# Vector-as-weights in four column tiles for two matrix-vector products at the edges of a decode kernel

## The chip, the cores and the metric

The kernel runs on one core of a Trainium2 chip (trn2). The metric is device time in microseconds (us). Before the change the median of the first three runs is 357.5 us (357.15 to 358.15). "Span" is the length of one profiled execution; the reported times are about 1.8 us longer. In the profiles PE is the matrix engine (PEld its weight loads), DVE the vector engine, ACT the scalar engine, and SPq and ACTq are the sync and the scalar engine issuing a transfer. The granted PE clock is the share of full speed at which the PE was let run; "half clock" is 0.50. PSUM (`ps`) is the memory that the matmuls here write to, in banks. "The tail" is what happens after the last big loads land, from about 342 us to the end.

## The reference, cut to what matters

```
q = x @ wq                                   # x: 1 x 512, 32 heads of 128
scores = q . k_cache ; p = softmax(scores)   # 8 KV heads, 32768 keys each
o = p . v_cache                              # 4096 numbers
a = o @ wo                                   # wo: 4096 x 512
b = (silu(x @ w_gate) * (x @ w_up)) @ w_down # w_down: 1792 x 512
g = sigmoid(sum(x * gate_w))
out = g * a + (1 - g) * b                    # 512 numbers, bf16
```

The K and V caches are 134 MB of the 148 MB that the kernel reads, so it is a kernel that streams memory. The products with wo and w_down multiply one vector by a matrix.

## The kernel before

All loads go through one queue into a ring of five slots. The order is wq, K, gate and up weights, K, w_down, then K and V halves in turn, then the last two V halves, then wo in four pieces (of 16, 8, 4 and 4 rows of matmuls). The last V half lands some 10 us before the last piece of wo.

The two products take a 128x128 block of the matrix as weights and one column of the vector as the moving operand. So the output lies down the partitions, as 128 x 4:

```python
# w_down, early in the kernel
for oc in range(OC):                      # OC = 4
    for j in range(FC):                   # FC = 14
        pe.matmul(ps_m[:, M_B0 + oc : M_B0 + oc + 1],
                  wd[:, j, oc * 128 : (oc + 1) * 128], tT[:, j : j + 1],
                  start=(j == 0), stop=(j == FC - 1))
# ... K and V stages cut ...
# wo, the last thing the PE does
for c, n in enumerate(WO_CUT):            # (16, 8, 4, 4)
    pe.wait_ge(sem_ldo[c], 16)            # that piece of wo has landed
    for j in range(j0, j0 + n):
        for oc in range(OC):
            ins = pe.matmul(ps_a[:, oc, :],
                            wo_v[:, j, oc * 128 : (oc + 1) * 128], O2[:, j : j + 1],
                            start=(j == 0), stop=(j == WOJ - 1))
    j0 += n
```

The combine step then works on 128 x 4, and a matmul with the identity and one more copy turn the result into four rows, which the store can write:

```python
dve.scalar_tensor_tensor(res, ps_a, g_col, b_pre, ALU.mult, ALU.add)   # 128 x 4
pe.matmul(ps_r[0:OC, 0:128], res[:, :], ident[:, :], start=True, stop=True)
dve.tensor_copy(row[:, :], ps_r[0:OC, 0:128])                          # 4 x 128
sp.dma_start(out[0, 0, :].rearrange("(c n) -> c n", c=OC), row[:, :])
```

## Time and profile before

| what | value | view |
|---|---|---|
| load queue | 97.2% of 16 engines' span | DMA queues |
| PE, DVE busy | 72%, 56% | page, part 1 |
| chain that ended last | DMA 67%, PE 29% | chain of waits |
| w_down: 56 matmuls | 1.55 us at 57 us | timeline |
| wo: 128 matmuls | 112 in 3.15 us, then a wait, then 16 in 0.58 us | timeline |

The page of the kernel before: granted PE clock and DMA share in 40 slices (tenths), the load queue, and the engines of the chain that ended last.

```profile
PEclk9999678978989896969899896969769987969656
DMA  8999999999999999999999999999999999999991
...
q1 hardware_dynamic: 5768, 148.11, 97.2%
...
DMA 67%; PE 29%; DVE 2%; issue 1%; SPq 0%; DVEq 0%
```

The loads never pause until the last slice. Only what stands behind the last landings can be exposed. The timeline of the tail, in order of time (start us, length us, engine, line, operation, and in brackets the idle time before it and what ended it):

```profile
342.74 3.21 PE L463 MATMUL ps<-ring,ET 128*16 128x512 bf16 x32 [5.41 <-DMA ring<-in_A_v_cache_dram]
...
346.81 1.05 PE L479 MATMUL ps<-osel,pv_sb 128*128 128x4 f32 x8 [0.86 <-DVE pv_sb L719]
...
348.87 3.15 PE L542 MATMUL ps<-O,ring 128*128 128x1 bf16 x112 [0.29 <-DVE O L765]
352.57 0.58 PE L542 MATMUL ps<-O,ring 128*128 128x1 bf16 x16 [0.56 <-DMA ring<-in_A_wo_dram]
353.31 0.22 DVE L769 SCALAR_TENSOR_TENSOR res<-ps,g_col,b_pre 128x4 bf16<-128x4 f32 x1 [4.50 <-PE ps L542]
353.58 0.27 PE L552 MATMUL ps<-ident,res 128*4 128x128 bf16 x1 [0.43 <-DVE res L769]
353.89 0.28 DVE L778 CAST row<-ps 4x128 bf16<-4x128 f32 x1 [0.36 <-PE ps L552]
354.19 0.34 SPq L329 DMA_DIRECT2D out_dram<-row  x1
```

Two paths meet in the tail. One starts where the last V half lands (342.7): P times V, a sum over groups (L479), a short vector chain, then the wo matmuls. The other is the landing of the last piece of wo. The PE had finished 112 of the 128 wo matmuls and sat idle 0.56 us until that piece landed.

### The profile page before, as it was taken

The numbers are of one execution on the slowest core, as the hardware profiler recorded it, in microseconds if no ns is written. First come the engines' busy times: TensorE is split into PE (matmuls) and PEld (weight loads), VectorE is DVE, ScalarE is ACT, GpSimd is POOL, SyncE is SP. The second block draws the span as 40 slices with busy tenths as digits, with TensorE's granted clock in tenths as the row PEclk, the third lists the DMA queues.
The fourth block names the chain that finished last, engine by engine and source line by source line (L and its number), as shares of the span: only waits on it lengthen the run. The fifth ranks groups of instructions, "written<-read, shape, count | busy, mean of one in ns | idle before, by whom it ended". The sixth has DMA issues, their size and how long they took to land.

```text
span 355.8 us, 6082 instructions
## 1 busy us (share of the span) xinstructions
PE 257.5 (72%) x2616; PEld 191.4 (54%) x2616; DVE 198.2 (56%) x372; ACT 14.5 (4%) x36; POOL 5.6 (2%) x22
## 2 busy tenths in 40 slices
PE   0439898869494967868593948868497929678735
PEld 0437887647382736655471828456474618365315
DVE  0239187928383764838392845748365927548401
ACT  1000011000100010000100010000100010000100
POOL 0200000000000000000000000000000000000000
PEclk9999678978989896969899896969769987969656
DMA  8999999999999999999999999999999999999991
GB/s 335 424 404 460 414 438 422 431 437 424 429 438 423 431 433 431 429 435 422 436 429 427 435 429 431 433 426 432 435 422 437 435 422 427 438 427 424 433 386 73
DMA packets 5797, 148.49 MB, mean 417 GB/s; under 512 B 650, under 2 KB 652, under 8 KB 908
## 3 DMA queue, kind: packets, MB, share of 16 engines
q1 hardware_dynamic: 5768, 148.11, 97.2%
q8 instruction: 20, 0.33, 0.4%
q14 instruction: 5, 0.04, 0.0%
q10 hardware_dynamic: 4, 0.00, 0.0%
HBM read 148.11 MB, written 0.00 MB: 416 GB/s over the span
## 4 chain that ended last, share of the span: by engine, by line
DMA 67%; PE 29%; DVE 2%; issue 1%; SPq 0%; DVEq 0%
DMA ring<-in_A_k_cache_dram 55%; PE ps L415 18%; DMA ring<-in_A_wo_dram 12%; PE ps L431 5%; PE ps L463 2%; PE ps L384 2%; DVE ktT L726 1%; PE ps L479 0%; PE ps L398 0%; SPq L317 0%; PE ps L445 0%; PE ps L542 0%; SPq L299 0%; PE ps L552 0%; DVE row L778 0%
## 5 line engine op out<-in xcount | busy, mean ns | idle before, releaser
L726 DVE COPY ktT<-ps 128x1024 bf16<-128x1024 bf16 x256 | 164.2, 685 | 104.4 <-PE ps L415 101.8
L415 PE MATMUL ps<-ident_f,ring 128*128 128x128 f32 x1024 | 164.3, 321 | 57.0 <-DMA ring<-in_A_k_cache_dram 57.0
L415 PEld LDWEIGHTS ps<-ident_f,ring 128*128 128x128 f32 x1024 | 141.0, 167 | 89.5 <-DMA ring<-in_A_k_cache_dram 63.6
L431 PE MATMUL ps<-ktT,qz 128*32 128x512 bf16 x512 | 41.8, 403 | 15.2 <-DVE ktT L726 15.1
L463 PE MATMUL ps<-ring,ET 128*16 128x512 bf16 x512 | 33.4, 406 | 5.4 <-DMA ring<-in_A_v_cache_dram 5.4
L463 PEld LDWEIGHTS ps<-ring,ET 128*16 128x16 bf16 x512 | 13.1, 94 | 22.2 <-DMA ring<-in_A_v_cache_dram 5.5
L431 PEld LDWEIGHTS ps<-ktT,qz 128*32 128x32 bf16 x512 | 7.9, 95 | 28.0 <-DVE ktT L726 24.4
L573 ACT ACTIVATE P<-ps,nbias 128x512 bf16<-128x512 f32 x16 | 10.8, 682 | 273.6 <-DVE nbias L703 273.6
L682 DVE TENSOR_REDUCE pmaxf<-ps 128x1 f32<-128x512 f32 x16 | 11.1, 692 | 11.9 <-PE ps L431 11.9
L479 PEld LDWEIGHTS ps<-osel,pv_sb 128*128 128x128 f32 x64 | 10.0, 237 | 1.7 <-DVE pv_sb L719 1.7
L479 PE MATMUL ps<-osel,pv_sb 128*128 128x4 f32 x64 | 9.6, 274 | 1.0 <-DVE pv_sb L719 0.9
L719 DVE COPY pv_sb<-ps 128x512 f32<-128x512 f32 x8 | 5.5, 682 | 8.3 <-PE ps L463 8.3
L289 POOL PARTITION_ALL_REDUCE gmax<-pmax x8 | 3.0, 373 | 310.5 <-DVE pmax L692 310.5
L445 PE MATMUL ps<-ident,P 128*128 128x128 bf16 x64 | 6.2, 219 | 1.8 <-ACT P L573 1.2
L711 DVE COPY ET<-ps 128x512 bf16<-128x512 bf16 x16 | 6.7, 416 | 1.3 <-PE ps L445 1.3
L384 PEld LDWEIGHTS ps<-xT,ring 128*128 128x128 bf16 x112 | 6.8, 159 | 0.4 <-issue 0.4
L384 PE MATMUL ps<-xT,ring 128*128 128x1 bf16 x112 | 6.9, 198 | 0.0
L359 PE MATMUL ps<-xT,ring 128*128 128x1 bf16 x128 | 3.6, 165 | 4.2 <-DMA ring<-in_A_wq_dram 4.2
L342 PE MATMUL ps<-ones_bf,x_row 1*128 1x1 bf16 x4 | 0.3, 172 | 8.3 <-DMA gw_row<-in_gate_w_dram 8.3
L445 PEld LDWEIGHTS ps<-ident,P 128*128 128x128 bf16 x64 | 4.8, 98 | 2.6 <-ACT P L573 2.4
L359 PEld LDWEIGHTS ps<-xT,ring 128*128 128x128 bf16 x128 | 3.5, 104 | 4.3 <-issue 4.3
L342 PEld LDWEIGHTS ps<-ones_bf,x_row 1*128 1x128 bf16 x4 | 0.2, 113 | 8.3 <-DMA gw_row<-in_gate_w_dram 8.3
(70 smaller groups left out, 38.1 us busy)
## 6 DMA issues: line engine op xcount, KB each, us to landing
ring<-in_A_k_cache_dram SPq DMA_DIRECT2D x16, 4096.0 KB, 43.0
ring<-in_A_v_cache_dram SPq DMA_DIRECT2D x16, 4096.0 KB, 36.9
ring<-in_A_wq_dram SPq DMA_DIRECT2D x1, 4096.0 KB, 13.4
ring<-in_A_wo_dram SPq DMA_DIRECT2D x1, 2048.0 KB, 38.3
ring<-in_B_w_gate_dram SPq DMA_DIRECT2D x1, 1792.0 KB, 26.7
ring<-in_B_w_up_dram SPq DMA_DIRECT2D x1, 1792.0 KB, 30.5
ring<-in_B_w_down_dram SPq DMA_DIRECT2D x1, 1792.0 KB, 43.5
ring<-in_A_wo_dram SPq DMA_DIRECT2D x1, 1024.0 KB, 40.4
```

Of the source, the lines that this page charges most:

```text
L359: ins = pe.matmul(ps_m[:, M_Q0 + h : M_Q0 + h + 1], wq_v[:, c, h * DH : (h + 1) * DH], xT[:, c : c + 1], start=(c == 0), stop=(c == KC - 1),)
L384: ins = pe.matmul(ps_m[:, base + j : base + j + 1], wt[:, c, :].rearrange("d (p j) -> d j p", j=FC)[:, j, :], xT[:, c : c + 1], start=(c = ...
L415: ins = pe.transpose(stb[:, t * 64 : (t + 2) * 64], two.bitcast(FP32), ident_f[:, :])
L431: ins = pe.matmul(ps_sc[f % NSC][32 * c : 32 * c + 32, :], qz[:, g, e, 24 - PB * i : 56 - PB * i], kt[:, e, :], start=(i == 0 and e == 0), ...
L445: ins = pe.transpose(ps_pt[:, (f % 2) * 512 + m * 128 : (f % 2) * 512 + (m + 1) * 128], P[:, f % 2, m * 128 : (m + 1) * 128], ident[:, :],)
L463: ins = pe.matmul(ps_pv[32 * c : 32 * c + 2 * PB, :], ET[:, f % NET, col : col + 2 * PB], src.rearrange("p (i c t) d -> p i c t d", i=NI, ...
L479: ins = pe.matmul(ps_m[:, M_OT + g * HPG : M_OT + (g + 1) * HPG], pv_sb[:, r * DH : (r + 1) * DH], osel[:, r * HPG : (r + 1) * HPG], start ...
L573: act.activation(P[:, f % 2, :], ps_sc[f % NSC], ACT.Exp, bias=nbias[:, f // 2 : f // 2 + 1], scale=SCALE, accum_out=esum[:, f // 2, f % 2 ...
L682: ins = dve.tensor_reduce(pmaxf[:, f : f + 1], ps_sc[f % NSC], AX.X, ALU.max)
L711: dve.tensor_copy(ET[:, f % NET, :], ps_pt[:, (f % 2) * 512 : (f % 2 + 1) * 512]).then_inc(sem_ptc, 1)
L719: dve.tensor_copy(pv_sb[:, :], ps_pv).then_inc(sem_pvc, 1)
L726: dve.tensor_copy(ktT[:, j % NKT, :], pst[j % NST]).then_inc(sem_cp, 1)
```

## The change

The intent: swap the operands of both products. The vector is now the weight, one column wide, and 128 columns of the matrix are the moving operand. The four output blocks run in four column tiles of the PE array, and the output lies in rows, on partitions 0, 32, 64 and 96. The combine step can then write rows, and the transposing matmul and the row copy go away. The combine now works on all 128 partitions though only four hold results, so the PSUM bank of the results is cleared at the start (the `memset` below).

```diff
-        b_pre = T("b_pre", [128, OC], FP32)
-        res = T("res", [128, OC], BF16)
-        row = T("row", [OC, 128], BF16)
+        b_pre = T("b_pre", [128, 128], FP32)
+        res = T("res", [128, 128], BF16)
...
-                sp.wait_ge(sem_row, 1)
+                sp.wait_ge(sem_res, 1)
                 sp.dma_start(
-                    out[0, 0, :].rearrange("(c n) -> c n", c=OC), row[:, :]
+                    out[0, 0, :].rearrange("(c n) -> c n", c=OC), res[0:128:32, :]
...                                       # w_down: the same swap, j now the outer loop
                             ins = pe.matmul(
-                                ps_a[:, oc, :],
+                                ps_a[32 * oc : 32 * oc + 1, :],
+                                O2[:, j : j + 1],
                                 wo_v[:, j, oc * 128 : (oc + 1) * 128],
-                                O2[:, j : j + 1],
...
-                pe.wait_ge(sem_res, 1)
-                pe.matmul(ps_r[0:OC, 0:128], res[:, :], ident[:, :], start=True, stop=True)
...
-                dve.memset(ps_pv, 0.0).then_inc(sem_pv0, 1)
+                dve.memset(ps[:, 6:8, :], 0.0).then_inc(sem_pv0, 1)
...
-                dve.tensor_copy(row[:, :], ps_r[0:OC, 0:128]).then_inc(sem_row, 1)
```

More of the change, by code (lines that the diff above doesn't have):

```diff
@@ L103, in bass_gated_mix__gqa_block_cached__swiglu_ffn__decode_kernel @@
         sem_pe_a = S_("s_pe_a")
-        sem_pe_r = S_("s_pe_r")
-        sem_row = S_("s_row")
         sem_xT = S_("s_xT")
@@ L197, in bass_gated_mix__gqa_block_cached__swiglu_ffn__decode_kernel @@
         ps_m = ps[:, 7, :]
-        ps_a = ps[:, 0:OC, 0:1]
-        ps_r = ps[:, OC, :]
         M_X0 = 0
@@ L205, in bass_gated_mix__gqa_block_cached__swiglu_ffn__decode_kernel @@
         M_B0 = M_U0 + FC
-        M_OT = M_B0 + OC
+        M_OT = M_B0
         M_O0 = M_OT + H
-        assert M_O0 + WOJ <= 512
+        M_BR = 256
+        M_AR = 384
+        assert M_O0 + WOJ <= M_BR
+        ps_b = ps_m[:, M_BR : M_BR + 128]
+        ps_a = ps_m[:, M_AR : M_AR + 128]
         def slot_of(entry):
@@ L338, in emit_x @@
                     pe.wait_ge(sem_ones, 2)
+                    pe.wait_ge(sem_pv0, 1)
                     for src, base in ((x_row, M_X0), (gw_row, M_X0 + KC)):
@@ L395, in emit_outb @@
                     pe.wait_ge(sem_tT, 1)
-                    for oc in range(OC):
-                        for j in range(FC):
+                    for j in range(FC):
+                        for oc in range(OC):
                             ins = pe.matmul(
-                                ps_m[:, M_B0 + oc : M_B0 + oc + 1],
+                                ps_b[32 * oc : 32 * oc + 1, :],
+                                tT[:, j : j + 1],
                                 wd[:, j, oc * 128 : (oc + 1) * 128],
-                                tT[:, j : j + 1],
                                 start=(j == 0),
@@ L453, in emit_pv @@
                     f = 2 * g + hf
-                    if hf == 0:
-                        pe.wait_ge(*((sem_pvc, g) if g > 0 else (sem_pv0, 1)))
+                    if hf == 0 and g > 0:
+                        pe.wait_ge(sem_pvc, g)
                     pe.wait_ge(sem_ptc, f + 1)
@@ L550, in _ @@
                 ins.then_inc(sem_pe_a, 1)
-                pe.wait_ge(sem_res, 1)
-                pe.matmul(
-                    ps_r[0:OC, 0:128], res[:, :], ident[:, :], start=True, stop=True
-                ).then_inc(sem_pe_r, 1)
             @block.scalar
@@ L676, in emit_bpre @@
                     dve.tensor_scalar(
-                        b_pre[:, :], ps_m[:, M_B0 : M_B0 + OC], omg[:, 0:1], None, op0=ALU.mult
+                        b_pre[:, :], ps_b, omg[:, 0:1], None, op0=ALU.mult
                     ).then_inc(sem_bpre, 1)
@@ L769, in _ @@
                 dve.scalar_tensor_tensor(
-                    res[:, :].unsqueeze(2),
+                    res[:, :],
                     ps_a,
                     g_col[:, 0:1],
-                    b_pre[:, :].unsqueeze(2),
+                    b_pre[:, :],
                     ALU.mult,
@@ L776, in _ @@
                 ).then_inc(sem_res, 1)
-                dve.wait_ge(sem_pe_r, 1)
-                dve.tensor_copy(row[:, :], ps_r[0:OC, 0:128]).then_inc(sem_row, 1)
 _INS = ['A_x', 'A_k_cache', 'A_v_cache', 'A_wq', 'A_wo', 'B_x', 'B_w_gate', 'B_w_up', 'B_w_down', 'gate_w']
```

## The prediction

> **What bounds the kernel now.** The load stream. The page's queue part gives the load queue 97.2% of 16 engines' span, at some 430 GB/s in the slices. The chain of waits puts 67% on DMA; PE is 72% busy, DVE 56%. The queue's own waits show 4 to 5 loads outstanding (36 to 43 us from issue to landing for 4 MB), so small changes of PE or DVE in the middle hardly reach the stream. Only what follows the last landing is exposed. The timeline of the end, in us:
>
> - 348.87 to 352.0: 112 of the 128 wo matmuls, behind the vector chain
> - 352.52: last piece of wo lands; 352.57 to 353.15: the last 16 matmuls
> - 353.31 to 353.53: combine (0.22)
> - 353.58: transposing matmul (0.27); 353.89 to 354.17: row copy (0.28)
> - 354.19: output DMA; 355.76: end of span
>
> **Removed.** The transposing matmul, the row copy and two handoffs: from the end of the combine (353.53) to the end of the copy (354.17), 0.64 us, all on the chain.
>
> **Added.** (a) The combine goes from 4 to 128 fp32 columns out of PSUM. Vector copies out of PSUM take 0.28 us at 128 columns and 0.69 at 512, so about 1.05 ns a column: +0.13 us, on the chain. (b) The last 16 matmuls now stream 128 columns instead of one. One matmul of 128 columns takes 0.27 us from start to end, of one column 0.165: +0.1 us at the end. (c) The same extra 0.13 us for the b_pre scaling, at 61 us, where DVE has slack; the PSUM clearing at the start doubles from 0.48 us, long over when x lands at 8.3 us. Both are free.
>
> **Moved: matmul rate.** The old wo matmuls follow each other at 27 ns (112 in 3.15 us). The Trainium skill (TensorEngine Tiling, Restrictions and Gotchas) says column tiling excludes fast weight load, but weights of one column need none. The last PV stage shows four column tiles starting within about 10 ns, a group of four every 427 ns for 512 columns at a low granted clock. A quarter of that is 107 ns per four matmuls, again 27 ns each. So I expect no gain in PE time from the tiling: 128 matmuls cost about what they did, w_down's 56 (1.55 us at 57 us) too. Both sit beside the load stream, which stays the same.
>
> **Sum.** -0.64 + 0.13 + 0.10 = -0.4 us, of 357.5: 357.1 us. Three runs of before spread over 1 us, so the median will hardly show it. I expect 357.1, range 356.2 to 357.9; faster by over 2% has a chance of 0.01, within 2% 0.98, slower 0.01.
>
> **What would show each step right or wrong.** In the tail of the timeline: no transposing matmul, no row copy; combine about 0.35 us; output DMA issued about 1.25 us after the last wo landing (before: 1.67). wo matmuls in 112s of about 3.0 to 3.3 us. Landing of the last wo piece within 1 us of 352.5, DMA share unchanged at 97%.
>
> **What would make it wrong.** If reloading the 1-column weights of a tile takes longer than its 107 ns of streaming, groups of four might need 145 ns. Then the first 112 take 4.1 us, end at 352.95, after the last landing, and the tail loses the gain (+0.35 us). The landing of the last piece itself depends on one straggling DMA engine (most wo packets end by 350.5, those of one engine at 352.1), so it can shift between runs. An output read from four partitions 32 apart instead of four neighbours might take a different time.

## The result, and the profile after

The changed kernel takes 357.62 us (median of 4 runs, 357.35 to 357.92), the kernel before 357.38 us beside it. The ratio is 1.0003, with a 95% interval of 0.9985 to 1.0022: the same. (A ratio is the mean time of one kernel's runs over that of the other's of the same rounds, so not quite the ratio of the medians quoted.) In the experiments the changed kernel ran again: 0.9994 (0.9981 to 1.0006). The narrower of the two intervals is some 0.45 us to each side, as large as the gain that was expected.

The same parts of the page, after:

```profile
PEclk9999789969859996989789798989698898989555
DMA  8999999999999999999999999999999999999991
...
q1 hardware_dynamic: 5768, 148.11, 97.2%
...
DMA 66%; PE 29%; DVE 3%; issue 2%; POOL 0%; SPq 0%; DVEq 0%
```

The load stream did not change. The timeline of the tail, after:

```profile
342.65 3.59 PE L463 MATMUL ps<-ring,ET 128*16 128x512 bf16 x32 [5.55 <-DMA ring<-in_A_v_cache_dram]
...
347.09 1.87 PE L479 MATMUL ps<-osel,pv_sb 128*128 128x4 f32 x8 [0.86 <-DVE pv_sb L715]
...
349.98 3.58 PE L542 MATMUL ps<-ring,O 128*1 128x128 bf16 x128 [0.28 <-DVE O L761]
353.73 0.35 DVE L765 SCALAR_TENSOR_TENSOR res<-ps,g_col,b_pre 128x128 bf16<-128x128 f32 x1 [3.80 <-PE ps L542]
354.11 0.63 SPq L328 DMA_DIRECT2D out_dram<-res  x1
```

Three things are to be seen. The transposing matmul and the row copy are gone, and the combine grew from 0.22 to 0.35 us. The issue of the store grew from 0.34 to 0.63 us. And the wo matmuls began 1.1 us later and no longer stopped for the last piece of wo: they ran 128 in one go. That piece landed at 352.45 us by the trace's landing records (352.52 before), when the PE was still busy, so the store began 1.66 us after the landing (1.67 before).

The last point goes with the clock. The windows of both kernels for the time around 345.4 to 348.8 us and after it: start and end, length, busy time and number of instructions of PE, PEld, DVE, ACT and POOL, then the granted PE clock, the DMA share and GB/s. First before, then after:

```profile
345.40:348.80 3.40, 1.79 (x21) 1.07 (x12) 1.28 (x4) 0.00 (x0) 0.00 (x0) 1.00 0.63 260
348.80:353.60 4.80, 3.75 (x129) 3.58 (x129) 0.23 (x2) 0.00 (x0) 0.00 (x0) 0.50 0.12 46
```

```profile
345.40:348.80 3.40, 2.54 (x16) 1.71 (x8) 0.69 (x1) 0.00 (x0) 0.00 (x0) 0.50 0.64 261
348.80:353.60 4.80, 3.96 (x130) 3.47 (x130) 0.59 (x3) 0.00 (x0) 0.00 (x0) 0.50 0.11 44
```

The execution of before had a full-clock stretch of 3.4 us in its tail, so the end of P times V and the sum (L479: 1.05 against 1.87 us) went faster. The changed one was at half clock from 331 us on. The ledger of the two tails, from these timelines (us; the end of the store's wait is the issue plus the wait in the queue's own waits, read from the trace's records):

| step | before | after |
|---|---|---|
| start of last P times V to first wo matmul | 6.13 | 7.33 |
| first wo matmul to combine | 4.44 (with the wait for wo) | 3.75 |
| start of combine to start of store | 0.88 | 0.38 |
| start of store to end of its wait | 1.19 | 1.65 |
| sum | 12.64 | 13.11 |

The two lower rows are the change itself: 0.50 us gained and 0.46 us given back. The two upper rows differ by 0.51 us, against the changed kernel. The experiments ask whether the 0.46 us belongs to the distance of the four partitions, and whether the clock difference belongs to the change.

### The profile page after: what moved, and what is told of

Read it like the earlier page. It is cut to its first block, busy times and chain, and to the rows that moved or that the text cites. A ratio compares the mean times of both kernels' runs of the same rounds, so it can differ in the third digit from the quotient of the medians.

```text
span 356.1 us, 6079 instructions
## 1 busy us (share of the span) xinstructions
PE 255.3 (72%) x2615; PEld 187.4 (53%) x2615; DVE 197.9 (56%) x371; ACT 14.5 (4%) x36; POOL 5.6 (2%) x22
## 3 DMA queue, kind: packets, MB, share of 16 engines
q1 hardware_dynamic: 5768, 148.11, 97.2%
## 4 chain that ended last, share of the span: by engine, by line
DMA 66%; PE 29%; DVE 3%; issue 2%; POOL 0%; SPq 0%; DVEq 0%
DMA ring<-in_A_k_cache_dram 56%; PE ps L415 17%; DMA ring<-in_A_v_cache_dram 10%; PE ps L431 5%; PE ps L463 3%; PE ps L384 2%; DVE ktT L722 2%; PE ps L479 1%; PE ps L542 1%; PE ps L445 0%; DVE pv_sb L715 0%; DVE pmaxf L678 0%; POOL gmax L288 0%; SPq L298 0%; DVE res L765 0%
## 5 line engine op out<-in xcount | busy, mean ns | idle before, releaser
L415 PE MATMUL ps<-ident_f,ring 128*128 128x128 f32 x1024 | 161.3, 316 | 59.8 <-DMA ring<-in_A_k_cache_dram 59.0
L415 PEld LDWEIGHTS ps<-ident_f,ring 128*128 128x128 f32 x1024 | 136.9, 164 | 93.7 <-DMA ring<-in_A_k_cache_dram 65.7
L479 PEld LDWEIGHTS ps<-osel,pv_sb 128*128 128x128 f32 x64 | 11.0, 258 | 2.1 <-DVE pv_sb L715 2.1
L479 PE MATMUL ps<-osel,pv_sb 128*128 128x4 f32 x64 | 10.7, 291 | 1.0 <-DVE pv_sb L715 0.9
```

Source lines behind the costliest of these rows:

```text
L415: ins = pe.transpose(stb[:, t * 64 : (t + 2) * 64], two.bitcast(FP32), ident_f[:, :])
L479: ins = pe.matmul(ps_m[:, M_OT + g * HPG : M_OT + (g + 1) * HPG], pv_sb[:, r * DH : (r + 1) * DH], osel[:, r * HPG : (r + 1) * HPG], start ...
```

## The experiments

Twelve kernels were run with five or six runs of each kernel. Kernels are compared only within the same rounds. The medians of the kernel before were 357.69, 357.39 and 357.27 us.

| label | built on | median us | ratio to before | 95% interval |
|---|---|---|---|---|
| after_again | changed | 357.45 | 0.9994 | 0.9981 to 1.0006 |
| near_out (wrong result) | changed | 356.95 | 0.9971 | 0.9959 to 0.9984 |
| far_out (wrong result) | before | 357.71 | 0.9999 | 0.9987 to 1.0012 |
| splitv_after | changed | 357.37 | 0.9982 | 0.9969 to 0.9996 |
| store4_after | changed | 357.34 | 0.9997 | 0.9983 to 1.0011 |
| warm_after | changed | 358.03 | 1.0016 | 0.9999 to 1.0033 |
| warm_before | before | 358.51 | 1.0027 | 1.0013 to 1.0042 |
| best1 | changed | 357.73 | 1.0005 | 0.9989 to 1.0020 |
| splitv_before | before | 357.30 | 0.9997 | 0.9983 to 1.0010 |
| store2_after | changed | 357.53 | 1.0006 | 0.9994 to 1.0019 |
| best2 | changed | 357.11 | 0.9994 | 0.9981 to 1.0007 |
| best3 | changed | 357.20 | 0.9999 | 0.9986 to 1.0011 |

### after_again: the changed kernel once more

No edit.

> The changed kernel once more, as the partner of the other runs of this call. Both theories: within 0.3% of the kernel before. Two theories of where the expected 0.4 us went. Theory D (output DMA): the store from four partitions 32 apart takes 0.63 us to issue against 0.34 and 1.65 us from issue to the end of its wait against 1.19, so it gives back 0.45 us; it should be seen again here, to within 0.05 us. Theory C (clock): the profiled changed run had the PE at half clock from 331 us to the end, the profiled run of before had a full-clock stretch from 345 to 349 us, so the changed run's wo products began 1.1 us later by chance. If C is chance, this profile may show either; if the change causes it, the PE is again at half clock for all of the tail.

The store was issued in 0.63 us again and its wait ended 1.65 us after its start. The PE was at half clock in the whole tail again, from the first wo matmul to the combine it took 3.75 us again, and the wo matmuls again ran 128 in one go. So the store is no accident. For the clock, two profiles of two is not enough; more follow below.

### near_out and far_out: only the distance of the four partitions

```diff
 # near_out, on the changed kernel (wrong result on purpose)
-   out[0, 0, :].rearrange("(c n) -> c n", c=OC), res[0:128:32, :]
+   out[0, 0, :].rearrange("(c n) -> c n", c=OC), res[0:OC, :]
 # far_out, on the kernel before (wrong result on purpose)
-   row = T("row", [OC, 128], BF16)
+   row = T("row", [128, 128], BF16)     # cleared at the start
-   out[0, 0, :].rearrange("(c n) -> c n", c=OC), row[:, :]
+   out[0, 0, :].rearrange("(c n) -> c n", c=OC), row[0:128:32, :]
```

> Changed kernel, output read from partitions 0 to 3 instead of 0, 32, 64, 96 (result wrong on purpose). Theory D: issue of the store falls from 0.63 to about 0.34 us, store start to end of wait from 1.65 to 1.19 us, time 0.45 us under the changed kernel. Rival (the partition distance is harmless, the 0.63 us is chance or belongs to something else in the new tail): store stays at 0.63 and 1.65 us, time as the changed kernel.

> Kernel before, its row copy unchanged in size, but the store reads partitions 0, 32, 64, 96 of a larger tile (result wrong on purpose). Theory D: issue rises from 0.34 to about 0.63 us, store to end of wait from 1.19 to 1.65 us, time 0.45 us over before. Rival: no change of the store.

The combine and the store of near_out, from its timeline, and then the wait after the store, from the queue's own waits (us in total, times, longest):

```profile
353.15 0.35 DVE L765 SCALAR_TENSOR_TENSOR res<-ps,g_col,b_pre 128x128 bf16<-128x128 f32 x1 [3.81 <-PE ps L542]
353.53 0.34 SPq L328 DMA_DIRECT2D out_dram<-res  x1
...
SPq L231 <- DMA out_dram<-res: 0.8, 1, 0.8
```

The same of far_out:

```profile
353.36 0.28 DVE L779 CAST row<-ps 4x128 bf16<-4x128 f32 x1 [0.36 <-PE ps L552]
353.67 0.64 SPq L329 DMA_DIRECT2D out_dram<-row  x1
...
SPq L232 <- DMA out_dram<-row: 1.0, 1, 1.0
```

Four neighbouring partitions: 0.34 us to issue, 1.19 us in all. Four partitions 32 apart: 0.63 to 0.64 us and 1.65 us, in the kernel before as well as in the changed one. One index expression moves this cost in and out, so the profiles show that it is the step from partition to partition (only 1 and 32 were tried). The trace's packets show where it lies: in both cases four packets of 256 bytes leave, at some 15 ns each, but the first leaves 0.77 us after the start of the store with neighbours and 1.23 us with distant partitions. What happens in that time no run shows. The times agree for near_out: all of its five runs (356.37 to 357.05) lie under all five of after_again (357.28 to 357.95). The difference of the means, 0.80 us, is more than the 0.46 us of the profile; in the two profiles the last V half also landed 0.26 us earlier in near_out (342.06 against 342.32), and that is not the store's doing. They do not confirm far_out: its mean is only 0.05 us over that of before (357.74 against 357.69). The runs of before in that call spread over 1.1 us, so 0.4 us could hide there, but it was not measured as time. In its profile the store costs 0.46 us more, and the last piece of wo lands 0.53 us earlier than in the profile of before (351.99 against 352.52), which hides it.

### splitv_after and splitv_before: less PE work after the last V byte

The last V half is loaded as two transfers, and the 32 P times V matmuls are ordered so that 16 need only the first.

```diff
+   if e == ("V", G - 1, 1):
+       sp.dma_start(dst[:, : RH // 2, :], src[:, : RH // 2, :]).then_inc(sem_vh, 16)
+       sp.dma_start(dst[:, RH // 2 :, :], src[:, RH // 2 :, :]).then_inc(sem_ld[i], 16)
+       continue
 ...
-   for m in range(NM):
-       for i0 in range(0, NI, 2):
+   order = [(m, i0) for i0 in range(0, NI, 2) for m in range(NM)]   # last V half only
+   for m, i0 in order:   # waits for sem_vh at i0 = 0, for the second part at i0 = 2
```

> Changed kernel, last V load in two halves with their own semaphores, so only 16 of 32 PV matmuls are left after the last V byte lands. Theory C with its consequence (in the profiled changed run the tail is bound by PE work after the last V landing: PV, sum, 128 wo matmuls at 27 ns, end of wo 1.1 us after the last wo landing): PV after the last landing 1.8 instead of 3.6 us, wo matmuls then wait for the last wo piece, time 0.3 to 0.6 us under the changed kernel and with less spread. Rival (the tail is bound by the last wo landing as the prediction had it): no change within 0.1 us.

> Kernel before with the last V load in two halves. Theory T (with the PE at half clock the tail of either kernel is bound by PE work after the last V landing, at full clock by the last wo landing): PV work after the last V landing falls from 3.2-3.6 to 1.9 us, the wo matmuls always wait for the last wo piece, and the time falls by 0.2 to 0.5 us against before, as splitv_after did against the changed kernel (0.4 us of medians less, within its interval). Rival (the split helps only the column-tiled kernel): no change.

The last P times V and the wo matmuls of splitv_after:

```profile
342.74 1.89 PE L477 MATMUL ps<-ring,ET 128*16 128x512 bf16 x16 [2.92 <-DMA ring<-in_A_v_cache_dram]
...
348.37 2.73 PE L557 MATMUL ps<-ring,O 128*1 128x128 bf16 x96 [0.28 <-DVE O L776]
351.32 0.60 PE L557 MATMUL ps<-ring,O 128*1 128x128 bf16 x16 [0.22 <-DMA ring<-in_A_wo_dram]
352.56 0.59 PE L557 MATMUL ps<-ring,O 128*1 128x128 bf16 x16 [0.65 <-DMA ring<-in_A_wo_dram]
353.33 0.35 DVE L780 SCALAR_TENSOR_TENSOR res<-ps,g_col,b_pre 128x128 bf16<-128x128 f32 x1 [5.01 <-PE ps L557]
```

P times V after the last landing fell to 1.89 us, still at half clock, and now the PE waits 0.65 us for the last piece of wo. So the profiled changed kernel was bound by PE work after the last V landing, and this one is bound by the landing of wo: at half clock the two paths are within about a microsecond of each other. In time, splitv_after is 0.3 us under after_again (means 357.21 and 357.54), as expected but not clear of the spread. splitv_before shows the same picture in its profile (a wait of 0.65 us ahead of the last 16 matmuls), but no gain in time (means 357.15 and 357.20, where 0.2 to 0.5 us was expected). That expectation missed; what the split is worth to the kernel before is not resolved.

### store4_after and store2_after: other ways to store four distant rows

```diff
 # store4_after: four one-partition stores, two from each of two engines
-   sp.dma_start(..., res[0:128:32, :]).then_inc(sem_out, 16)
+   for oc in (0, 1):          # sync engine; the scalar engine does (2, 3)
+       sp.dma_start(out_rows[oc : oc + 1, :], res[32 * oc : 32 * oc + 1, :]).then_inc(sem_out, 16)
 # store2_after: two two-partition stores
+   sp.dma_start(out_rows[0:2, :], res[0:64:32, :]).then_inc(sem_out, 16)     # sync engine
+   act.dma_start(out_rows[2:4, :], res[64:128:32, :]).then_inc(sem_out, 16)  # scalar engine
```

> Changed kernel, its store cut into four stores of one partition each, two from the sync engine and two from the scalar engine (result correct). Theory D1 (the 0.63 us of the changed store belong to one transfer that steps over partitions 32 apart): each of these is issued in 0.2 to 0.35 us, the last of two is issued by 0.55 us after the combine, and the end comes 0.1 to 0.2 us sooner than with the one store. Rival D2 (any second store costs as much as the step): no gain, or a loss of up to 0.3 us.

> Changed kernel, store cut into two stores of two partitions each (still 32 apart), one from the sync engine and one from the scalar engine. In store4_after each one-partition store took 0.22 to 0.31 us to issue, and two on one engine together about as long as the one stepped store, with no gain. If stepping costs about 0.1 us for each partition beyond the first (0.34 for neighbours, 0.63 for four apart), each issue here takes some 0.4 to 0.45 us and start of store to end of wait falls from 1.65 to about 1.4 us, 0.2 us of time. If the step costs a fixed 0.29 us whatever the count, the issue stays at 0.63 us and nothing is gained.

The stores of store4_after, from its timeline (two on each engine, merged):

```profile
353.54 0.64 SPq L330 DMA_DIRECT2D out_dram<-res  x2
353.55 0.52 ACTq L582 DMA_DIRECT2D out_dram<-res  x2
```

The stores of store2_after:

```profile
353.14 0.61 SPq L329 DMA_DIRECT2D out_dram<-res  x1
353.14 0.58 ACTq L578 DMA_DIRECT2D out_dram<-res  x1
```

A one-partition store takes 0.22 to 0.31 us to issue, but two in a row take 0.64 us on the sync engine, as long as the stepped one, and 0.52 us on the scalar engine. A store of only two partitions 32 apart takes 0.61 us, nearly the 0.63 us of four. So the cost of the step is the same for two and for four partitions, about 0.29 us of issue, and not per partition: the guess of 0.1 us per partition fell. From the start of the store to the end of the wait the two variants take 1.62 and 1.85 us, against 1.65 us. Neither gains.

These two profiles also answer the question of the clock. Both have a full-clock stretch in the tail. The windows of store2_after:

```profile
345.40:348.80 3.40, 1.73 (x25) 1.21 (x25) 1.29 (x4) 0.00 (x0) 0.00 (x0) 0.84 0.62 257
348.80:353.60 4.80, 2.70 (x128) 1.83 (x118) 0.35 (x1) 0.00 (x0) 0.00 (x0) 0.61 0.11 44
```

Of the changed kernel and its variants that alter only the store, three profiles were at half clock through the tail (the first, after_again, near_out) and two had a full-clock stretch of 3.4 us (store4_after, store2_after). Their work up to the combine is identical, so the clock of the tail varies from execution to execution. From the start of the last P times V to the combine, the three took 11.08, 11.08 and 11.09 us and the two 10.59 and 10.61 us. The old kernel with its stretch took 10.57 us in both of its profiles. So the 0.51 us of the ledger's upper rows goes with the clock: with such a stretch, old and new kernel reach the combine equally fast. Both profiles of the unsplit old kernel (before, far_out) had one as well. That the late start of the wo matmuls came with the change is therefore not supported; that the old kernel meets the fast stretch no more often than the new one is not shown either, with two profiles against five.

The clock records narrow it down. In all 14 profiles the clock changes only at borders that lie multiples of 3.41 us apart, and every rise followed a 3.41 us window with at least 2.68 us of PE work (a full window alone is not enough: in before, 331.77 to 335.19 us was busy throughout and half clock followed). Of the seven unsplit profiles, the four with a stretch have a border 2.7 to 4.3 us after the start of the last P times V, and the window that ends there holds 2.68 to 3.36 us of PE work. The three without have borders about 1.7 and 5.1 us after that start, and none of their windows from there to the combine holds more than 2.60 us. The P times V work is the same in both kernels. So what separates the two groups is where a border falls; no run shows the old kernel with a border as in the three.

The stretch in store2_after, from 346.5 to 349.9 us by the trace's clock records, also reaches into the wo matmuls:

```profile
348.66 1.65 PE L541 MATMUL ps<-ring,O 128*1 128x128 bf16 x96 [0.28 <-DVE O L763]
350.75 0.60 PE L541 MATMUL ps<-ring,O 128*1 128x128 bf16 x16 [0.45 <-DMA ring<-in_A_wo_dram]
351.99 0.59 PE L541 MATMUL ps<-ring,O 128*1 128x128 bf16 x16 [0.65 <-DMA ring<-in_A_wo_dram]
```

96 wo matmuls took 1.65 us here and 2.73 us in splitv_after, at half clock. The starts of the groups of four lie 55 ns apart at full clock, as in the w_down product, and 107 ns apart at half. What that gained was lost again in the wait for the last pieces of wo.

### warm_after, warm_before, best1: filler matmuls to hold the clock up

```diff
+   def warm(n):      # 128x512 matmuls into an unused PSUM bank
+       for _ in range(n):
+           pe.matmul(ps[:, 2, :], ident[:, :], ktT[:, 0, 0:512], start=True, stop=True)
 ...
+   warm(2)           # before the wait for the first part of the last V half
+   warm(6)           # before the wait for its second part
+   warm((0, 0, 3, 3)[c])   # before the waits for the last two pieces of wo
```

All three are built on the split V load. warm_before writes to bank 5 instead of bank 2, and best1 adds the four stores and wo in pieces of 16, 8, 6, 2.

> Changed kernel with the last V load in two halves (as splitv_after) and filler matmuls into an unused PSUM bank in the waits of the tail, to keep the PE at full clock. Theory P (column tiles make the wo matmuls faster only at full clock; the w_down products show 13 to 14 ns per matmul at full clock, the wo products 27 ns at half): wo matmuls at 13 to 15 ns each, the 112 or so ahead of the last landing take about 1.6 us, and the last 16 take 0.36 instead of 0.59 us. As they end behind the last wo landing, the time falls by only 0.2 us against splitv_after. Rival (the rate is set by issue or weight loads, not by the clock): 27 ns at full clock too. If the granted clock stays at one half, the run tells nothing of P.

> Kernel before with the same two edits as warm_after (filler into another free bank). Theory P: the old wo matmuls, whose moving side is one column, stay at 26 to 28 ns each at full clock, the last 16 at 0.58 us. Rival: they get faster with the clock as well, to some 14 ns. Time as before or up to 0.3 us under it.

> Changed kernel with split last V load, filler matmuls, four one-partition stores and the last wo piece cut from four rows of matmuls to two (pieces 16, 8, 6, 2). If the parts add up: 0.4 (tail off the PE) + 0.2 (clock) + 0.15 (store) + 0.1 (smaller last piece), so 0.6 to 0.9 us under the changed kernel, 356.7 us, 0.2% under before, which 5 rounds should just resolve. If the landing of the last wo piece is all that counts, only the store and the last piece gain, 0.25 us, unresolved.

All three became slower or stayed as they were. The fillers held the clock up for one 3.4 us window longer: in warm_after it was full from 336.2 to 343.05 us, and in store2_after, without fillers, from 336.2 to 339.65 us. (The rise itself came before the first filler, whose weights were loaded at 336.43 us.) But in both warm profiles it was back at one half by 345 us. In warm_after the window before the fall, 339.64 to 343.05 us, held only 0.96 us of PE work, and its longest idle time was 2.45 us. Most of the wo stage ran at half clock after all, and there the fillers stood in the way. The end of warm_after's wo stage:

```profile
352.27 0.60 PE L566 MATMUL ps<-ring,O 128*1 128x128 bf16 x16
...
352.80 1.05 PE L342 MATMUL ps<-ktT,ident 128*128 128x512 bf16 x3
...
353.77 0.39 PE L566 MATMUL ps<-ring,O 128*1 128x128 bf16 x16
```

Three fillers of up to 427 ns each sit between the last two pieces. The last piece had landed at 352.34 us, so the last 16 matmuls began 1.4 us late. Of the wo matmuls only these 16 ran at full clock (it rose at 353.29 us): 0.39 us, where the expectation had 0.36 instead of 0.59. For the rest these runs tell nothing of how the wo matmuls would run at full clock, as the expectation of warm_after says; the profile of store2_after and the w_down product do that instead.

### best2 and best3: what adds up

```diff
-   WO_CUT = (16, 8, 4, 4)
+   WO_CUT = (16, 8, 6, 2)
```

best2 is splitv_after with this cut, best3 is best2 with the two stores of store2_after.

> Changed kernel with the last V load in two halves and wo in pieces of 16, 8, 6, 2, without fillers and with its own store. If both add up: 0.4 us (split) + 0.2 us (8 matmuls left behind the last landing instead of 16) under the changed kernel, 0.2% under before. If the next to last piece, now larger, lands so late that its 24 matmuls queue behind it, only the split gains.

> best2 with the store of store2_after. If the two stores help as said there, another 0.2 us under best2, 0.3% under before in all; if not, as best2.

The last wo matmuls of best2:

```profile
351.31 1.02 PE L557 MATMUL ps<-ring,O 128*1 128x128 bf16 x32 [0.85 <-DMA ring<-in_A_wo_dram]
```

In best2 the last two pieces ran as this one group of 32 matmuls, with no wait between them: when the large piece was done the small one had already landed. So 32 matmuls, not 16, stood behind the last wait. best2 is 0.9994 of before, best3 0.9999, both within the interval. No version was shown to beat the kernel before beyond the spread, except by a hair splitv_after (0.9969 to 0.9996), which best2, with the same split, did not confirm.

## Why the prediction was right or wrong

The forecast of 357.1 us, 356.2 to 357.9, "within 2%" at 0.98, held: 357.62 us. That says little for its steps: the range is 1.7 us wide, four times the expected gain, and would have held with no gain at all. The expected gain of 0.4 us did not show, and the reasons can be told one by one. With the terms as measured below, the sum is -0.64 + 0.13 + 0.03 + 0.46 = -0.02 us.

- **Bound by the load stream: right.** The load queue's share is 97.2% in both profiles.
- **Removed 0.64 us, combine +0.13 us: right.** The combine took 0.35 us as forecast, and start of combine to start of store fell from 0.88 to 0.38 us, a gain of 0.50 us.
- **The sum lacked the store.** This is the step that failed. The prediction named "an output read from four partitions 32 apart instead of four neighbours" among its risks but left it out of the sum. It costs 0.46 us: issue 0.34 to 0.63 us, start to end of wait 1.19 to 1.65 us. near_out takes it away, far_out brings it into the kernel before. It cancels the 0.50 us.
- **"+0.1 us at the end" for the last 16 matmuls: too much, it is 0.03.** Start of the last group to start of the combine was 0.74 us before and 0.77 us in splitv_after, where the same 16 also start at a landing. A matmul of 128 columns is longer, but the old group with its 128-column weights was not faster as a whole.
- **"no gain in PE time from the tiling": right at half clock, wrong at full clock.** The prediction scaled a half-clock figure (107 ns per group of four) and held it against 27 ns per old matmul, as if the clock were the same everywhere. The old form hardly profits from the clock: the 56 w_down matmuls ran in a full-clock stretch and still started 25 ns apart, against 27 ns for the wo matmuls at half clock. The new form does profit; the timelines of w_down, before and then after:

```profile
57.22 1.55 PE L398 MATMUL ps<-tT,ring 128*128 128x1 bf16 x56
```

```profile
56.38 0.96 PE L398 MATMUL ps<-ring,tT 128*1 128x128 bf16 x56
```

  The starts of the groups of four lie 55 ns apart, so 14 ns per matmul. This gain of 0.6 us lies beside the load stream and does not reach the time. The Trainium skill (TensorE: Matmul & The Clock Gate, Back-to-back issue gap) gives N / 2.4 + 2.5 ns for one isolated matmul of N columns at full clock, its weight load not counted, about 56 ns for 128; the trace shows 55 ns for four such matmuls in four tiles, weight loads included. It also puts a matmul with 1 to 64 columns at a floor of about 25 ns; the old form shows 25 ns at full clock, and 27 ns at half.
- **The risk that "groups of four might need 145 ns": did not happen.** Groups followed each other at 107 ns at half clock, a quarter of the 427 ns of the 512-column groups. The Trainium skill (TensorEngine Tiling, Restrictions and Gotchas) says only that column tiling excludes fast weight load; that one-column weights don't need it was the prediction's own step, and the 107 ns bear it out.
- **"output DMA issued about 1.25 us after the last wo landing": right only where the landing binds.** In splitv_after the store started 1.15 us after the last 16 matmuls were released (352.56 to 353.71). In the profiled changed run the PE was late and the landing did not bind: the store started 1.66 us after it. The lateness goes with the clock. The Trainium skill (TensorE: Matmul & The Clock Gate, Part 1) says that the PE clock falls to one half after an idle window of about 3.4 us and rises after a busy one, and that these windows run free of the kernel. The trace agrees in part: the granted clock takes only the values 1.0 and 0.5 and changes after multiples of 3.4 us. But it falls without an idle window: in before it fell at 331.77 us after 3.41 us in which the PE was busy for 1.48 us. Whether a full-clock window falls into the tail moves the start of the wo matmuls by 0.8 to 1.2 us (6.13 to 6.51 us after the start of the last P times V, against 7.33) and the combine by 0.5 us. That is as large as the effect to be found.

So the explanation is: the change saves 0.50 us in the tail (profiles), pays 0.46 us for its store (shown by near_out and far_out in the profile, by near_out also in time), and the remaining differences go with the clock and the landing of the last load, which vary between executions.

## What to carry to other kernels

Where a kernel is bound by its load stream, cost a change to its end as a chain through to the landing of the output, and look up the store too: its partitions are part of the layout choice. A new form that only matches the old one at half clock may be twice as fast at full clock, so read rates together with the granted clock. When two paths end within a microsecond of each other, taking 0.5 us off one of them mostly moves the wait.

## What the Trainium skill lacked or had wrong

- DMA: Bandwidth & Descriptors has no figure for a source whose partitions lie apart. A store of four rows of 256 bytes took 0.34 us to issue from neighbouring partitions and 0.63 us from partitions 32 apart, and 0.61 us already for two such partitions (0.58 us from the scalar engine); a single-partition store took 0.22 to 0.31 us. So the step costs the same for two and for four partitions.
- DMA: Bandwidth & Descriptors (Anatomy of one DMA) puts the fixed cost of a DMA of the other, GPSIMD-driven kind at about 2.0 us, and has no such sum for a DMA that the sync engine issues; these small stores, issued by the sync engine, took 1.19 us from start of issue to the end of the wait with neighbouring partitions and 1.65 us with distant ones.
- TensorEngine Tiling has no rate for one-column weights with 128 moving columns in four column tiles: 107 ns per group of four at half clock and 55 ns at full clock, with no gap for the weight reloads.
- TensorE: Matmul & The Clock Gate advises against idle gaps over 3.4 us, but shorter ones are enough for the clock to fall: in warm_after it fell to half at 343.05 us with no PE gap over 2.45 us and 0.96 us of PE work in the 3.41 us before, in before at 331.77 us with no gap over 1.2 us and 1.48 us of work. Nor does a window full of work always raise it: in before, 331.77 to 335.19 us was busy throughout, and half clock followed.
